# Six norm operations for eight, an inverse on its column factors, and a re-set opening schedule in a fused attention and MoE kernel

## The chip, the cores and the metric

The kernel runs on one core of a Trainium2 chip. Its time is the device time of one execution in microseconds. Three runs of the kernel before gave 586.13, 586.37 and 587.09 us, median 586.37. One profiled execution took 586.01 us, of which the trace shows a span of 584.3 us. TensorE's granted clock is given as a share of 2.4 GHz: 1.00 is 2.4 GHz, 0.50 is 1.2 GHz.

## The reference, cut to what matters

Delta-rule attention for 4 batches and 8 heads over 768 steps with 48 dimensions, and then a two-layer MLP with a squared ReLU on the 3072 rows it gives. `w_in` and `w_out` come as 64-bit floats.

```python
k_n = k / (np.linalg.norm(k, axis=-1, keepdims=True) + 1e-06)
for t in range(S):
    kt, vt, bt = k_n[:, :, t], v[:, :, t], beta[:, :, t, None]
    y[:, :, t] = np.einsum('bhd,bhde->bhe', q[:, :, t], state)
    v_old = np.einsum('bhde,bhd->bhe', state, kt)
    state = state + bt[:, :, :, None] * np.einsum('bhd,bhe->bhde', kt, vt - v_old)
h = np.maximum(x @ w_in, 0.0)          # x: y as 3072 x 384, w_in 384 x 2048
out = (h * h @ w_out).astype(np.float32)
```

## The kernel before, in words

The 768 steps are cut into 12 units of 64, and two units make a pair. Within a unit the recurrence is solved at once: the products of the keys with each other are formed on TensorE, their triangular system is inverted, and TensorE applies the inverse to the values. Two units are prepared together, because their 32 x 32 diagonal blocks are laid out so that one VectorE stream transpose brings all of them into rows (tile `lt`). The inverse is built by substitution, one column per step, two VectorE operations per step.

The first pair (`pair < FAST`) has a shorter path. Its 32 x 32 blocks are inverted as two 16 x 16 blocks each (`invert` on `z16`, 15 steps), scaled by beta over the squared norm (`ended`), transposed into `t1` (L571) and `tt` (L566), and the quarter between the two 16-blocks is then filled in by `corrected`: a first group of products (L588), a scaling with row masks (L594, L597), a second group (L607), a subtraction (L611) and two transposes (L613). `below` then fills the quarter between the two 32-blocks in the same manner (L623, L624, then L633, L634, negated at L638 and L640). `state_part` applies the result to the values (L783), turns the output to the layout of the MLP (`turned_y`, L729) and updates the state (L802).

Products of 64 rows can be put on one of four quarters of the 128 x 128 array: the half of the rows is set by where the inputs lie, the half of the columns by where the output lies. In L588 and L607 inputs and output lie in the same half, which uses two quarters. L430, L688 and L783 also send one head of each pair to the opposite half, which uses all four.

Norms (`prepare`): a square root on ScalarE (L480), then eight small VectorE operations (L485 to L495) for one step of refinement, the division and the beta factor.

The MLP multiplies in two parts per operand, a high and a low half, so each weight has to be split once (`split_weights`): 17 tiles are loaded as 64-bit words, cast on ScalarE or VectorE (L253, into `rest`), joined on VectorE (L279, into `a`), rounded to the high half (L285 or L287), and subtracted for the low half (L269), or, where the table `mode` says P, multiplied by the identity and its negative on TensorE (L265, tile 1 alone). L875 is the first layer, L882 to L885 the squared ReLU and the high half of its result, L850 the low half, L859 the second layer.

All queues are in order and written by hand. In the opening, the string `order` gives the pieces one by one, `fill` and `fillm` say how many weight steps go behind each piece, `loads` the order of the first loads and `ahead` how far weight loads run ahead of the casts. From unit 1 on, pieces of attention are woven into the MLP of the unit before at the fractions in the tables. SP issues every load; a load waits in SP's queue for its buffer, and what stands behind it waits too. Load `kp` (L323) waits for the state update, values `vt` for the end of what used their buffer (in the first pair `goff`, the input of L588), `kb` for the transposes on TensorE that read it (L380).

Of the kernel before, what the change touches and what calls it, by code (L numbers as in the profile page):

```python
# [22 lines left out]
def kernel(  # L23
# [20 lines left out]
              'keys': [0.0259, 0.1552],  # L44
              'm0': 0.0875,
              'm1': 0.9358,
              'prepare': [0.4739, 0.3325],
# [4 lines left out]
              'update': [0.0],  # L52
              'v1': [0.1099, 0.2455],
              'values': [0.2013, 0.7593]},
          2: {'end': 0.0,
              'ended': [0.4457, 0.4449, 0.5557, 0.3799],
              'inverse': [0.042, 0.3114],
              'keys': [0.4933, 0.4581],
              'm0': 0.0151,
              'm1': 0.7158,  # L60
              'out': 0.3937,
# [4 lines left out]
          'ahead': 2,  # L66
# [13 lines left out]
                   'steps': [0.2072, 0.4146, 0.4716, 0.511, 0.6399],  # L80
                   'values': [0, 0.749]},
          'fill': [0, 0, 0, 0, 0, 0, 0, 0, 0, 0, 0, 0, 0, 0, 0, 0, 0, 0, 0, 0, 0, 0, 0, 0, 0, 0, 0, 0, 0, 0, 0, 0, 0, 0, 0,
                   0, 0, 0, 0, 0, 0, 1, 0, 0, 4, 2, 2, 2, 1, 0, 2, 2],
          'fillm': [0, 0, 0, 0, 0, 0, 0, 0, 0, 0, 0, 0, 0, 0, 0, 0, 0, 0, 0, 0, 0, 0, 0, 0, 1, 0, 0, 0, 0, 0, 1, 0, 0, 0, 0,
                    0, 0, 0, 0, 0, 0, 0, 0, 2, 2, 0, 1, 0, 0, 0, 1, 1],
# [3 lines left out]
          'homes': {'0': 'o', '1': 'o', 'b0': 'h', 'c0': 'o', 'k0': 'h', 'k1': 'g', 'w': 'h', 'y': 'o'},  # L89
          'kk': 0,  # L90
          'last': [1, 1],
          'loads': 'kKvbwcwqr',
          'mode': ['AAD', 'AAP', 'AAD', 'AAD', 'AAD', 'AAD', 'AAD', 'AAD', 'AAD', 'AAD', 'AAD', 'DDD', 'AAD', 'AAD', 'AAD',
                   'AAD', 'ADD'],
          'neg': 'DA',
          'odd': {'end': 0.0,
                  'inverse': [0.458, 0.9654],
                  'keys': [0.2429, 0.0785],
                  'm0': 0,
                  'm1': 0.9003,  # L100
                  'out': 0.1651,
                  'prepare': [0.3057, 0.4746],
                  'queries': [0.5785, 0.9867],
                  'rows': [0.9443],
                  'steps': [0.2902, 0.4708, 0.7443, 0.9418],
                  'values': [0.2259, 0.4952]},
          'order': '0A1lBATPPxB2PPPPPPPIGVIIAIBIIIIIIIIIIIeeeGZecccbbyss',
# [3 lines left out]
          'turn': 'DDAAA',  # L111
          'upper': 'DD',
# [245 lines left out]
    def spread_beta():  # L358
# [4 lines left out]
        for i in range(2):  # L363
            for s in range(2):
# [755 lines left out]
```

## Time and profile before

| | us |
|---|---|
| median of three runs | 586.37 |
| profiled execution | 586.01 |
| its span | 584.3 |
| TensorE busy, share of the span | 548.6, 94% |
| VectorE busy | 363.8, 62% |
| ScalarE busy | 318.1, 54% |
| first product of the MLP (L875) | starts at 55.89 |
| last product of the MLP (L900) | ends at 580.5 |

The span is the time from the first to the last recorded instruction, and 1.7 us of the execution lie outside it. A matmul of 32-bit floats shows twice in the trace, so 32 products of the program are 64 records. A busy TensorE at a clock of 0.50 does the same work as at 1.00 in up to twice the time, so its busy share has to be read beside the clock. The opening, to about 92 us, is a chain through all engines; behind it TensorE hardly stops.

### The profile page before, as it was taken

Reading aid. Unit: us, or ns where it says so; the run is one execution under the profiler, and the core shown is the slowest. Engines: PE = TensorE matmul, PEld = TensorE weight load, DVE = VectorE, ACT = ScalarE, POOL = GpSimd, SP = SyncE. Lnnn points to the kernel's source line nnn. Section 1 sums busy time; section 2 is a strip of 40 time slices with the busy share of each in tenths; the row PEclk is TensorE's granted clock in tenths of the full one; section 3 lists DMA queues with packets and bytes.
Section 4 is the critical chain, followed back from the end, with each engine's and each line's share of the span. In section 5 each row is a group of like instructions: output and inputs, shape, how many; then the busy total and the mean of one; then the engine's idle time right before and its main releaser. Section 6 shows DMA issues by size and latency. Waiting matters only on the chain.

```text
span 584.3 us, 20855 instructions
## 1 busy us (share of the span) xinstructions
PE 548.6 (94%) x9344; PEld 525.1 (90%) x9344; DVE 363.8 (62%) x699; ACT 318.1 (54%) x540; POOL 50.5 (9%) x62
## 2 busy tenths in 40 slices
PE   5377869999999999999999999999999999999997
PEld 4366859999899999999999999999999999999997
DVE  1887888995358795458795458794459793420210
ACT  4277876456374455474455474455474455454533
POOL 5110002001002002002001002001002010000000
PEclk9559999999999999999999999999999999999999
DMA  9882970322350230460331450321450320200101
GB/s 172 220 346 51 258 157 2 75 37 30 55 85 2 53 59 14 60 96 2 65 47 15 63 93 2 70 42 19 65 87 2 76 35 4 57 2 2 28 1 27
DMA packets 146793, 37.62 MB, mean 64 GB/s; under 512 B 140400, under 2 KB 143472, under 8 KB 146704
## 3 DMA queue, kind: packets, MB, share of 16 engines
q1 hardware_dynamic: 146624, 36.19, 31.0%
q8 instruction: 73, 1.20, 0.9%
q14 instruction: 16, 0.13, 0.1%
q10 hardware_dynamic: 80, 0.10, 0.0%
HBM read 31.55 MB, written 4.72 MB: 62 GB/s over the span
## 4 chain that ended last, share of the span: by engine, by line
PE 83%; SPq 3%; ACT 2%; DMA 1%; DVE 1%; issue 0%; DVEq 0%; ACTq 0%
PE h L875 34%; PE o L859 31%; PE g L764 3%; PE g L776 2%; PE g L859 2%; PE g L819 2%; PE g L783 2%; SPq L235 2%; PE g L802 1%; PE g L430 1%; PE h L834 1%; SPq L323 1%; DMA w<-in_moe_w_out_dram 1%; PE g L900 1%; PE g L663 1%; PE g L651 1%
## 5 line engine op out<-in xcount | busy, mean ns | idle before, releaser
L859 PE MATMUL o<-w,h_h 128*128 128x384 f32 x704 | 183.7, 341 | 1.2 <-issue 1.1
L875 PE MATMUL h<-x_h,w 128*128 128x256 f32 x1152 | 171.8, 285 | 3.2 <-ACT r L882 3.2
L875 PEld LDWEIGHTS h<-x_h,w 128*128 128x128 f32 x1152 | 153.5, 190 | 6.7 <-ACT r L882 3.7
L850 DVE TENSOR_TENSOR h_l<-r,h_h 128x512 fp32r<-128x512 f32 x96 | 66.4, 692 | 132.9 <-ACT h_h L885 132.9
L859 PEld LDWEIGHTS o<-w,h_h 128*128 128x128 f32 x704 | 122.3, 188 | 4.1 <-issue 1.7
L859 PE MATMUL o<-w,h_l 128*128 128x384 f32 x352 | 118.3, 336 | 1.9 <-DVE h_l L850 1.9
L882 ACT ACTIVATE r<-h 128x512 f32<-128x512 f32 x96 | 57.7, 601 | 104.2 <-PE h L875 92.1
L875 PE MATMUL h<-x_l,w 128*128 128x256 f32 x576 | 100.2, 283 | 0.0
L875 PEld LDWEIGHTS h<-x_l,w 128*128 128x128 f32 x576 | 82.6, 191 | 0.0
L859 PEld LDWEIGHTS o<-w,h_l 128*128 128x128 f32 x352 | 66.1, 188 | 2.6 <-DVE h_l L850 2.5
L883 ACT ACTIVATE r<-r 128x512 f32<-128x512 f32 x96 | 60.8, 633 | 3.1
L885 ACT CAST h_h<-r 128x512 fp32r<-128x512 f32 x96 | 59.6, 621 | 3.0
L541 DVE TENSOR_TENSOR tmp<-lt 128x30 f32<-128x30 f32 (+9 forms) x150 | 53.2, 355 | 3.5
L543 DVE TENSOR_TENSOR lt<-lt,tmp 128x30 f32<-128x30 f32 (+9 forms) x150 | 51.7, 344 | 5.8 <-DVE tmp L541 0.5
L677 POOL TENSOR_SCALAR_AFFINE_SELECT ap<-ap 64x1024 f32<-64x1024 f32 x24 | 33.0, 1374 | 222.0 <-ACT ap L767 219.3
L805 DVE TENSOR_TENSOR qs<-qs,g 48x768 f32<-48x768 f32 x22 | 20.9, 950 | 15.2 <-PE g L802 15.0
L767 ACT COPY ap<-g 128x512 f32<-128x512 f32 x22 | 11.9, 590 | 31.2 <-DVE vt L766 31.0
L482 POOL TENSOR_SCALAR_AFFINE_SELECT lt<-lt 128x1024 f32<-128x1024 f32 x5 | 6.3, 1267 | 219.6 <-ACT s L480 161.9
L822 ACT COPY y<-g 128x768 f32<-128x768 f32 x11 | 8.8, 801 | 27.6 <-PE g L819 27.6
L764 PE MATMUL g<-qs,kt 48*64 48x112 f32 x704 | 19.4, 259 | 0.0
L764 PEld LDWEIGHTS g<-qs,kt 48*64 48x64 f32 x704 | 17.0, 133 | 1.7 <-issue 0.5
L253 ACT CAST rest<-w 128x768 f16<-128x768 bf16 (+1 forms) x16 | 16.4, 1022 | 3.5 <-DMA w<-in_moe_w_out_dram 3.2
(176 smaller groups left out, 617.1 us busy)
## 6 DMA issues: line engine op xcount, KB each, us to landing
w<-in_moe_w_out_dram SPq DMA_DIRECT2D x16, 383.8 KB, 8.2
vt<-in_v_dram SPq DMA_DIRECT2D x48, 96.0 KB, 4.4
kp<-in_k_dram SPq DMA_DIRECT2D x48, 96.0 KB, 3.1
w<-in_moe_w_in_dram SPq DMA_DIRECT2D x6, 767.8 KB, 9.0
out_dram<-rest SPq DMA_DIRECT2D x47, 96.0 KB, 2.2
kb<-in_q_dram SPq DMA_DIRECT2D x40, 64.0 KB, 3.2
kb<-in_k_dram SPq DMA_DIRECT2D x32, 64.0 KB, 2.7
w<-in_moe_w_in_dram SPq DMA_DIRECT2D x3, 511.8 KB, 7.1
```

Of the source, the lines that this page charges most:

```text
L253: (nc.vector.tensor_copy if A["mode"][x][0] == "D" else nc.scalar.copy)(out=head.bitcast(F16)[:, 1::2], in_=raw.rearrange("p n w -> p (n w ...
L541: nc.vector.tensor_tensor(out=tmp, op=ALU.mult, in0=z[:, s:s + 1, s + 1:].broadcast_to([P, nj, nt]), in1=z[:, :nj, s:s + 1].broadcast_to([ ...
L543: nc.vector.tensor_tensor(out=z[:, :nj, s + 1:], in0=z[:, :nj, s + 1:], in1=tmp, op=ALU.add)
L677: nc.gpsimd.affine_select(out=half, in_=half, pattern=[[0, 2 * X], [1, C]], base=0, channel_multiplier=-1, compare_op=ALU.is_gt, fill=0.0)
L764: nc.tensor.matmul(ps[half_rows(b ^ j), j, x], lhsT=kts[u][dims(j), n], rhs=qs[dims(j), n], start=True, stop=True)
L805: nc.vector.tensor_tensor(out=s[dims(j)], in0=s[dims(j)], in1=ps[dims(j)], op=ALU.add)
L850: nc.vector.tensor_tensor(out=h_l, in0=r, in1=h_h.bitcast(F32), op=ALU.subtract)
L859: nc.tensor.matmul(o[i], lhsT=a[:, e, i * P:(i + 1) * P], rhs=w_[w], start=(ft == 0 and n == 0), stop=(ft == FT - 1 and n == 2))
L875: nc.tensor.matmul(hp[:, e], lhsT=half_of(("wi", kt, part))[w][:, f], rhs=x[:, kt], start=(n == 0), stop=(n == 3 * KT - 1))
L882: nc.scalar.activation(out=r, in_=hp, func=AF.Relu)
L883: nc.scalar.activation(out=r, in_=r, func=AF.Square)
L885: nc.scalar.copy(out=h_h, in_=r)
```

## The change

The schedule table is set anew, and the first pair is computed with fewer and smaller operations:

- Norms: the maximum is replaced by a small bias inside the square root; half the root plus the epsilon is formed by a second ScalarE operation, and one VectorE operation adds the refined half. Six VectorE operations remain.
- The inverse starts from the scaled diagonal (`bt` is written there) and is multiplied by the factor of its column from the start, so the two scalings in `ended` go.
- `t1` of the first pair is transposed for the first 16 rows of each block only.
- `corrected` works on 16 columns where it worked on 32, and sends the second head of each pair to the opposite column half. Its scaling for that head becomes four operations on 64 rows, its subtraction three operations where there was one. Two zeroed tiles `w` and `y` take the scaled result.
- Table: `loads` puts the first weight third and the values behind two weights; `ahead` is 4, not 2; tile 1 of the weights no longer goes through TensorE (`mode`); the copies named in `turn`, `neg` and `upper` move partly from VectorE to ScalarE; `fill` and `fillm` put weight steps earlier.

```diff
-          'ahead': 2,
+          'ahead': 4,
-          'loads': 'kKvbwcwqr',
+          'loads': 'kKwbwcvqr',
-          'neg': 'DA',
+          'neg': 'AA',
-          'turn': 'DDAAA',
-          'upper': 'DD',
+          'turn': 'ADAAA',
+          'upper': 'AD',
...
-        nc.scalar.activation(out=s0, in_=n2, func=AF.Sqrt)
+        nc.scalar.activation(out=s0, in_=n2, func=AF.Sqrt, bias=tiny)
+        nc.scalar.activation(out=n1, in_=s0, func=AF.Copy, scale=0.5, bias=1e-6)
...
-        nc.vector.tensor_scalar(out=s1, in0=s0, scalar1=1e-30, scalar2=None, op0=ALU.max)
-        nc.vector.reciprocal(out=s1, in_=s1)
+        nc.vector.reciprocal(out=s1, in_=s0)
         nc.vector.tensor_tensor(out=s1, in0=s1, in1=n2, op=ALU.mult)
-        nc.vector.tensor_tensor(out=s1, in0=s1, in1=s0, op=ALU.add)
-        nc.vector.tensor_scalar(out=n1, in0=s1, scalar1=0.5, scalar2=1e-6, op0=ALU.mult, op1=ALU.add)
+        nc.vector.scalar_tensor_tensor(out=n1, in0=s1, scalar=0.5, in1=n1, op0=ALU.mult, op1=ALU.add)
...
         if d["pair"] < FAST:
             z = z32
-            for h in range(2):
-                r = slice(h * QB, (h + 1) * QB)
-                nc.vector.tensor_tensor(out=z[:, r, r], in0=z16[:, h], in1=bt[:, r].unsqueeze(1).broadcast_to([P, QB, QB]),
-                                        op=ALU.mult)
-                yield
...
-        nc.vector.transpose(out=t1.rearrange("p j i x s -> p s (j i x)"), in_=z.rearrange("p s t -> p (s t)"))
+        ns = HB if d["pair"] else QB
+        nc.vector.transpose(out=t1[..., :ns].rearrange("p j i x s -> p s (j i x)"),
+                            in_=z[:, :ns].rearrange("p s t -> p (s t)"))
...
-                    nc.tensor.matmul(ps[j][r, 0, x], lhsT=goff[r, j, x].rearrange("p n t -> p (n t)"), rhs=t1[r, j, i, x],
+                    nc.tensor.matmul(ps[j][half_rows(b ^ j), 0, x, :QB], lhsT=goff[r, j, x].rearrange("p n t -> p (n t)"), rhs=t1[r, j, i, x, :QB],
                                      start=True, stop=True)
...
-                    nc.tensor.matmul(ps[r, j, 0, x], lhsT=yt[j][r, x].rearrange("p n s -> p (n s)"), rhs=z[r, j, x],
+                    nc.tensor.matmul(ps[half_rows(b ^ j), j, 0, x, QB:], lhsT=yt[j][r, x].rearrange("p n s -> p (n s)"), rhs=z[r, j, x, QB:],
                                      start=True, stop=True)
...
-        nc.vector.tensor_tensor(out=z[:, :, :, QB:], in0=z[:, :, :, QB:], in1=ps[:, :, 0, :, QB:], op=ALU.subtract)
+        nc.vector.tensor_tensor(out=z[:, 0, :, QB:], in0=z[:, 0, :, QB:], in1=ps[:, 0, 0, :, QB:], op=ALU.subtract)
+        for b in range(2):
+            part = z[half_rows(b), 1, :, QB:]
+            nc.vector.tensor_tensor(out=part, in0=part, in1=ps[half_rows(1 - b), 1, 0, :, QB:], op=ALU.subtract)
```

On VectorE, between the scaling in the first `corrected` and its subtraction, stand weight steps (`a` joins a weight, `w_...` is its low half). Before:

```order
L594 TENSOR_SCALAR tmp<-o,rows 128x8x32 x2
L279 SCALAR_TENSOR_TENSOR a<-w_142,rest 128x768
L269 TENSOR_TENSOR w_464<-a,w_464 128x768
L279 SCALAR_TENSOR_TENSOR a<-w_224,rest 128x768
L611 TENSOR_TENSOR tt<-tt,g 128x2x8x16
L613 STREAM_TRANSPOSE t_410<-tt 128x256 x2
```

And now, with the line numbers of the changed kernel:

```order
L601 TENSOR_SCALAR y<-o,rows 64x8x16 x4
L280 SCALAR_TENSOR_TENSOR a<-w_126,rest 128x768
L280 SCALAR_TENSOR_TENSOR a<-w_132,rest 128x768
L270 TENSOR_TENSOR w_459<-a,w_459 128x768
L280 SCALAR_TENSOR_TENSOR a<-w_217,rest 128x768
L617 TENSOR_TENSOR tt<-tt,g 128x8x16
L620 TENSOR_TENSOR tt<-tt,g 64x8x16 x2
L622 STREAM_TRANSPOSE t_373<-tt 128x256 x2
```

Four weight steps stand there instead of three, and the scaling and the subtraction are in more pieces.

On TensorE, between the second group of `corrected` (L607) and the first of `below` (L623), stood the low half of weight tile 1:

```order
L607 MATMUL g<-tt,tmp 64x32 x2
L265 MATMUL g<-a,eye 128x384
L265 MATMUL g<-w_468,minus 128x384
L265 MATMUL g<-a,eye 128x384
L265 MATMUL g<-w_468,minus 128x384
L623 MATMUL g<-tt,mt 32x32
L624 MATMUL g<-t_410,mt 32x32
```

Now the two groups stand back to back:

```order
L613 MATMUL g<-tt,w 64x16 x2
L613 MATMUL g<-tt,y 64x16 x2
L632 MATMUL g<-tt,mt 32x32
L633 MATMUL g<-t_373,mt 32x32
```

The four products of 384 columns have left the engine; their subtraction is done on VectorE.

On SP, the loads from weight tile 9 on, counted from 0 (`kb` keys of unit 3, `kp` keys by rows, `vt` values, `w_...` weights). Before:

```order
L235 DMA w_241<-in_moe_w_out_dram 128x1535 x2
L329 DMA kb<-in_k_dram 64x16x48 x2
L323 DMA kp<-in_k_dram 64x8x48 x4
L235 DMA w_892<-in_moe_w_out_dram 128x1535 x2
L323 DMA vt<-in_v_dram 64x8x48 x4
L235 DMA w_1006<-in_moe_w_out_dram 128x1535 x2
L235 DMA w_1015<-in_moe_w_in_dram 128x2047
L235 DMA w_1035<-in_moe_w_in_dram 128x2047
L235 DMA w_1043<-in_moe_w_in_dram 128x2047
L323 DMA vt<-in_v_dram 64x8x48 x4
L235 DMA w_1056<-in_moe_w_out_dram 128x1535 x2
L235 DMA w_1076<-in_moe_w_out_dram 128x1535 x2
```

And now:

```order
L236 DMA w_237<-in_moe_w_out_dram 128x1535 x2
L236 DMA w_240<-in_moe_w_out_dram 128x1535 x2
L330 DMA kb<-in_k_dram 64x16x48 x2
L324 DMA vt<-in_v_dram 64x8x48 x4
L236 DMA w_787<-in_moe_w_out_dram 128x1535 x2
L324 DMA kp<-in_k_dram 64x8x48 x4
L236 DMA w_862<-in_moe_w_in_dram 128x2047
L236 DMA w_906<-in_moe_w_in_dram 128x2047
L236 DMA w_1014<-in_moe_w_in_dram 128x2047
L236 DMA w_1034<-in_moe_w_out_dram 128x1535 x2
L236 DMA w_1043<-in_moe_w_out_dram 128x1535 x2
L324 DMA vt<-in_v_dram 64x8x48 x4
```

One more weight tile stands ahead of the keys of unit 3, and the second load of values stands behind the last weight instead of ahead of the last two.

On ScalarE, the cast of the first weight now stands between the copies of the transposed keys of unit 1 and the second copies of `z`; before, the first cast stood behind the copy of the query products (L691).

## Rows read from the trace of the kernel before

**Rows 1.** Page, part 4: shares of the chain that ended last, by engine.

```profile
PE 83%; SPq 3%; ACT 2%; DMA 1%; DVE 1%; issue 0%; DVEq 0%; ACTq 0%
```

**Rows 2.** Windows: stretch, then busy us of each engine, clock, DMA share, GB/s.

```profile
44.00:56.00 12.00, 8.63 (x458) 7.68 (x458) 7.99 (x12) 8.49 (x14) 0.00 (x0) 1.00 0.22 43
...
56.00:92.00 36.00, 28.61 (x526) 25.74 (x527) 29.25 (x43) 29.44 (x50) 1.27 (x1) 1.00 0.71 175
...
92.00:584.00 492.00, 486.94 (x7999) 470.95 (x7997) 298.00 (x579) 258.87 (x435) 36.57 (x31) 1.00 0.24 41
```

**Rows 3.** Chain of waits, 60 to 100 us: start us, us, what.

```profile
75.93 5.06 DMA w<-in_moe_w_out_dram
...
81.07 1.04 ACT rest L253
```

**Rows 4.** Timeline of VectorE, 15 to 43 us: start us, us, operation [idle before].

```profile
17.30 0.18 DVE L485 TENSOR_SCALAR s<-s 128x32 f32<-128x32 f32 x1 [0.32 <-ACT s L480]
...
29.79 0.76 DVE L555 TENSOR_TENSOR w<-w,bt 128x256 f32<-128x256 f32 x2
...
30.59 1.99 DVE L571 STREAM_TRANSPOSE t<-w 128x1024 f32<-128x1024 f32 x1
...
37.18 0.95 DVE L279 SCALAR_TENSOR_TENSOR a<-w,rest 128x768 int32<-128x768 int32 x1
...
40.78 0.42 DVE L611 TENSOR_TENSOR tt<-tt,g 128x256 f32<-128x256 f32 x1 [0.39 <-PE g L607]
```

**Rows 5.** Timeline of TensorE, 27 to 57 us.

```profile
27.49 1.99 PE L688 MATMUL g<-qs,kt 48*64 48x64 f32 x64 [1.16 <-ACT kt L385]
...
32.72 3.62 PE L588 MATMUL o<-t,vt 64*64 64x32 f32 x64 [3.25 <-DVE t L571]
...
37.06 0.42 PE L607 MATMUL g<-tt,m 64*64 64x32 f32 x4 [0.72 <-ACT m L597]
...
40.66 1.65 PE L265 MATMUL g<-a,eye 128*128 128x384 f32 x2
...
44.13 0.21 PE L623 MATMUL g<-tt,mt 32*32 32x32 f32 x1
...
47.12 1.27 PE L783 MATMUL h<-vt,tt 64*64 64x48 f32 x64
...
53.94 2.02 PE L588 MATMUL g<-t,vt 64*64 64x32 f32 x64
...
55.89 0.97 PE L875 MATMUL h<-x_h,w 128*128 128x256 f32 x6
```

**Rows 6.** Windows of 1 us, for the granted clock.

```profile
16.00:17.00 1.00, 0.00 (x0) 0.00 (x0) 0.97 (x1) 0.31 (x1) 0.00 (x0) 0.87 0.95 336
...
39.00:40.00 1.00, 1.00 (x24) 1.00 (x22) 1.00 (x2) 1.00 (x2) 0.00 (x0) 0.50 0.99 396
...
44.00:45.00 1.00, 0.88 (x65) 0.64 (x64) 0.61 (x1) 0.76 (x2) 0.00 (x0) 0.98 0.00 0
```

**Rows 7.** Timeline of ScalarE: the second copies of z, the negations.

```profile
12.73 0.37 ACT L442 COPY z<-g 128x256 f32<-128x256 f32 x1 [1.25 <-PE g L430]
...
46.19 0.78 ACT L640 ACTIVATE tt<-h 32x256 f32<-32x256 f32 x2
```

**Rows 8.** DMA issues begun between 6 and 10 us, last column us to landing.

```profile
w<-in_moe_w_in_dram SPq DMA_DIRECT2D x1, 767.8 KB, 4.9
```

**Rows 9.** Timeline of the SP queue, 54 to 62 us.

```profile
54.13 3.13 SPq L323 DMA_DIRECT2D kp<-in_k_dram  x4
...
58.51 3.29 SPq L323 DMA_DIRECT2D vt<-in_v_dram  x4
```

**Rows 10.** Waits between 56 and 92 us: us, times, longest.

```profile
PE h L875 <- ACT r L882: 3.2, 2, 2.7
...
PE o L859 <- DVE h_l L850: 1.9, 2, 1.2
...
PE g L633 <- ACT m L626: 1.8, 1, 1.8
```

More of the change, by code (lines that the diff above doesn't have):

```diff
@@ L43 @@
               'inverse': [0.4545, 0.9674],
-              'keys': [0.0259, 0.1552],
-              'm0': 0.0875,
+              'keys': [0.0259, 0.15],
+              'm0': 0.0942,
               'm1': 0.9358,
-              'prepare': [0.4739, 0.3325],
+              'prepare': [0.4761, 0.3194],
               'queries': [0.945, 0.8623],
@@ L51 @@
               'steps': [0.3132, 0.5592, 0.7964, 0.8486],
-              'update': [0.0],
-              'v1': [0.1099, 0.2455],
-              'values': [0.2013, 0.7593]},
+              'update': [0.0647],
+              'v1': [0.2624, 0.2455],
+              'values': [0, 0.7871]},
           2: {'end': 0.0,
-              'ended': [0.4457, 0.4449, 0.5557, 0.3799],
+              'ended': [0.3926, 0.4449, 0.5557, 0.3799],
               'inverse': [0.042, 0.3114],
               'keys': [0.4933, 0.4581],
-              'm0': 0.0151,
+              'm0': 0.0164,
               'm1': 0.7158,
-              'out': 0.3937,
+              'out': 0.3959,
               'queries': [0.6885, 0.6959],
@@ L356, in load_beta @@
                 nc.sync.dma_start(out=brows[r0:r0 + X], in_=by[j, b * X:(b + 1) * X])
+    yts = []
     def spread_beta():
@@ L370, in spread_beta @@
         nc.scalar.copy(out=betas, in_=global_ps.rearrange("p (d t) -> p d t", t=HB))
+        for name in ("w", "y"):
+            y = apool.tile([P, XD * 2], F32, name=name)[:, :X * C].rearrange("p (x n s) -> p x n s", x=X, n=2)
+            nc.gpsimd.memset(y[..., QB:].rearrange("p x n s -> p (x n) s"), 0.0)
+            yts.append(y)
         return betas
@@ L587, in corrected @@
                     r = half_rows(b)
-                    nc.tensor.matmul(ps[j][r, 0, x], lhsT=goff[r, j, x].rearrange("p n t -> p (n t)"), rhs=t1[r, j, i, x],
+                    nc.tensor.matmul(ps[j][half_rows(b ^ j), 0, x, :QB], lhsT=goff[r, j, x].rearrange("p n t -> p (n t)"), rhs=t1[r, j, i, x, :QB],
                                      start=True, stop=True)
-        yt = [apool.tile([P, 2 * X * HB], F32, name=name).rearrange("p (x n s) -> p x n s", x=X, n=2) for name in ("m", "tmp")]
+        yt = yts
         for j in range(2):
             for n in range(2):
-                if j and A["yt"][i] == "D":
-                    nc.vector.tensor_scalar(out=yt[j][:, :, n], in0=ps[j][:, 0], scalar1=rows[:, 2 + n:3 + n], scalar2=None,
-                                            op0=ALU.mult)
-                else:
-                    nc.scalar.mul(out=yt[j][:, :, n], in_=ps[j][:, 0], mul=rows[:, 2 + n:3 + n])
+                for b in range(1 + j):
+                    to, of = (half_rows(b), half_rows(1 - b)) if j else (slice(P), slice(P))
+                    dst, src, by = yt[j][to, :, n, :QB], ps[j][of, 0, :, :QB], rows[to, 2 + n:3 + n]
+                    if j and A["yt"][i] == "D":
+                        nc.vector.tensor_scalar(out=dst, in0=src, scalar1=by, scalar2=None, op0=ALU.mult)
+                    else:
+                        nc.scalar.mul(out=dst, in_=src, mul=by)
         if not i:
```

44 lines of the change are left out of this document (23 added, 21 removed).

## The prediction

> **What bounds the kernel now.** I read the shares of the chain that ended last first: TensorE holds 83% of it [rows 1]. The windows say where it does not. From 92 us to the end of the span TensorE is busy for 486.9 of 492.0 us, and most of the 5.1 us left is the tail behind its last product; from 56 to 92 us it is busy for 28.6 of 36.0 [rows 2]. So time won in the opening is kept to the end, at the same amount, and time won off TensorE's path later is worth nothing. The chain of waits shows what holds the stretch to 92 us: it runs through the loads, and the last weight lands at 75.93 + 5.06 = 81.0 us, with its cast on ScalarE right behind, at 81.07 [rows 3]. The waits of that stretch show the price: TensorE stood for 3.2 + 1.9 + 1.8 = 6.9 us for results of ScalarE and VectorE [rows 10], engines that are in order and were standing behind casts of weights not yet there. Before 56 us the chain is the arithmetic of the first pair; its steps are in the timelines of VectorE and TensorE [rows 4, 5].
>
> **The first pair, up to its correction.** Two VectorE operations of 0.18 us go from the norms, about 0.4 with their gaps; the added ScalarE operation runs beside the reciprocal. The two scalings behind the inverse go: 29.79 to 30.59, 0.8. The transpose to `t1` halves: 1.99 to 1.0, an estimate by its elements; the bounds are 1.99 and 0.8. Together 2.2, so the correction begins at 30.5 instead of 32.72 [rows 4, 5]. The later pairs keep their own scaling, and their shorter norms lie beside a busy TensorE: nothing.
>
> **The two groups of products.** The first took 3.62 us at a clock of 0.50, and the second ran from 37.06 to 40.66 [rows 5], 3.6. No row has 16 columns on four quarters. The nearest are on four quarters with more columns: 64 records of 64 columns in 1.99 us in the same slow stretch, and 64 of 48 columns in 1.27 at full clock, where the same kernel's own two-quarter group of 32 columns took 2.02 [rows 5]. So fewer than 2.0 and no more than 3.6; I take 2.0, by the nearest row, 1.6 off each group.
>
> A rule speaks against this. The Trainium skill ("TensorE: Matmul & The Clock Gate", Part 3, The mechanism) says that a weight load overlaps a running product only when the two use different row groups, and the column half, which is what changes here, does not enter. By that rule both groups stay at 3.6. The rows above disagree: 48 columns on four quarters were faster than 32 on two. I go by the rows and keep the rule as a rival.
>
> **Scaling, subtraction and what stands between.** Four scalings for two, and three subtractions of half the columns for one of 0.42 [rows 4]: between 0 and 0.9 each; I take 0.4 and 0.5. The second group then ends at 30.5 + 2.0 + 1.3 + 2.0 = 35.8 against 40.7. VectorE is the later one now: it has four weight steps of about 0.9 [rows 4] between scaling and subtraction, so the subtraction begins at 33.8 + 3.6 = 37.4 and the transposes end at about 39.1, where they ended at 42.0. The next group of TensorE had to wait further, behind the four products of L265, from 40.66 to 44.13 [rows 5]; they are gone. So it begins at 39.1: **5.0 us earlier**, and what VectorE has in their place (one subtraction, 0.9) lies behind it.
>
> **The clock.** This is what I hold against the 5.0. The granted clock fell to 0.50 near 17 us, when TensorE had been without work; it was still 0.50 in the microsecond from 39 to 40, with TensorE busy throughout on the second group; and it was 0.98 from 44 to 45 [rows 6], right behind the four 128 x 384 products that the change removes. What raised it before is therefore not there any more, and the products now standing from 30 to 56 us are small ones with waits between. I expect 1.2 GHz up to the MLP. Between 44 and 56 us TensorE did 8.6 us of work at full clock [rows 2]. The 64 records of 32 columns took 3.62 against 2.02, 1.8 times as long [rows 5]. Of the 8.6, the second unit's first correction group (2.02) gets its four quarters and stays at about 2.0; some 1.0 of transposes runs beside other waits; the remaining 5.6 grow by 0.8 of themselves, 4.5. The negation for the second head moves from VectorE to ScalarE, behind the first, which takes 0.78 [rows 7]; between 0 and 0.8 of it is new on the path, since VectorE's own ended a little later than ScalarE's, and I take 0.5. So the MLP's first product comes at 55.89 - 5.0 + 4.5 + 0.5, about where it was. At the half clock the MLP then does half its work until the clock returns; between 0 and 4 us are lost, I take 2.0. The second unit's second correction group loses columns and halves in the same way: 0.8 won.
>
> The Trainium skill's section on the clock gate in the same page (Part 1) has the engine throttled by default and released by activity; the trace agrees in that small products at 39 us had not released it.
>
> **The loads.** SP's queue was blocked before by the `kp` load, which waited for the state update until 54.13; then keys, a weight, values, a weight, three narrow weights, values and two weights went out [rows 9], 27 us until 81.0. Now one more weight is out before, values stand behind the first correction of unit 1 (near 53.5), and the second values stand behind the last weight. By 768 KB a weight [rows 8] and the sizes in the order, about a fifth of the bytes is gone from that stretch, so the last weight lands near 53.5 + 21.5 = 75, 6 us earlier, or near 71.5 where the row loads cost more than their bytes. ScalarE and VectorE no longer stand behind missing weights, and of the 6.9 us of waits [rows 10] I take 6.0 as gone. VectorE has room: 29.3 of 36.0 busy [rows 2]. Its next limit, if the loads come, is that list of weight steps itself, and TensorE's own work: 28.6 us in that stretch cannot shrink.
>
> **Sum.** 0.0 at the first MLP product, -2.0 clock, +0.8, +6.0: 4.8 us. Against the profiled execution 586.01 - 4.8 = 581.2; the median of the runs is 0.36 above it, so **581.4 us**. By the unknowns (groups of products, pieces, clock, waits) from 579 to 584.
>
> **Rivals.**
>
> *The clock comes back early.* If the products on four quarters, or those of the turn (L729), bring 2.4 GHz back before the MLP, the 4.5 and the 2.0 are not paid, and the second unit's first group is 0.9 shorter; of this some 2.0 is given back, because VectorE's weight steps then end later than TensorE needs them. Gain 4.8 + 4.5 + 2.0 + 0.9 - 2.0 = 10.2, about 576. For it: TensorE no longer waits 3.5 us for itself. Against: the microsecond from 39 to 40.
>
> *The quarters give nothing.* Both groups stay at 3.6: the second ends at 39.0, the subtraction and transposes at 40.7, 1.6 later, and unit 1 loses its 0.8. Gain 4.8 - 1.6 - 0.8 = 2.4, 584. The rule of the skill named above would have it so.
>
> *The waits stay.* The loads come earlier, but VectorE's list of splits, which was 81% busy in that stretch, has no place to move to, and TensorE waits for low halves (L850) as before. Then 6.0 falls to about 0.5: 0 - 2.0 + 0.8 + 0.5, a loss of 0.7 against 586.4: 587, no change.
>
> *Slower: the half clock lasts into the MLP.* The MLP's first 36 us are woven with small products and waits, and each microsecond at 0.50 loses half a microsecond of its work. The gains behind 56 us, 6.8, are used up after 14 us at half clock, that is when the clock is not back by 70; to 80 it would be 591. For it: the same windows. Against: the MLP's products are of the large kind that stood before the rise at 44. A second way to it, the cast of the first weight on ScalarE, does not decide: it stands ahead of copies that began at 12.73 [rows 7], the weight is now issued right behind the two loads of keys with which the program begins, and before it landed 4.9 us after its issue with loads ahead of it as well [rows 8]; each microsecond by which it makes the copies late costs one.
>
> **Chances.** Forecast (579 to 584) 0.47; clock back early (574 to 579) 0.24; no help from quarters, or smaller gains to 585.2, 0.11; waits stay, within 0.2% (585.2 to 587.5, what a measurement here can tell from no change) 0.07; slower 0.11. Faster 0.82, same 0.07, slower 0.11. The range of 8 in 10 leaves out half of each end: 575.5 to 585.4.
>
> **What would show it.** In the changed profile: L592's first group at about 30.5 for 2.0 us (3.6: the quarters give nothing); L632 at 39; the clock in the windows from 40 to 56 (0.50: forecast; 1.00: first rival); the first product of L884 at 55 to 56, or 51; the last cast of a weight at 71 to 76; and TensorE's waits from 56 to 92 at about 1 us. I am wrong in the mechanism if the last weight still lands at 81, or if TensorE has new idle time behind 92 us.

## The result, and the profile after

The changed kernel took 577.61 us (median of four runs, 576.72 to 578.85) beside 586.73 us (586.13 to 587.90) for the kernel before on the same chip: ratio 0.985, 95% interval 0.982 to 0.987. That is faster, by 9.1 us where the forecast's sum had 4.8. It lies inside the range of 8 in 10 (575.5 to 585.4), but below the forecast's own band (579 to 584), in the band that was given to an early return of the clock (574 to 579); that rival is not what happened, as the clock below shows. The profiled execution took 578.17 us with a span of 576.4, 7.9 below that of before; the steps below are counted in spans.

The chain that ended last (page, part 4, shares by engine) is now TensorE for 91%, before it was 83% with 3% of SP's queue [rows 1]:

```profile
PE 91%; DVE 5%; DMA 1%; ACT 1%; issue 1%; SPq 0%; DVEq 0%
```

The windows (busy us of PE, PEld, DVE, ACT and POOL, then clock, DMA share, GB/s), in the same stretches as [rows 2]:

```profile
44.00:56.00 12.00, 9.25 (x389) 8.02 (x388) 11.51 (x17) 10.37 (x21) 0.00 (x0) 0.64 0.58 135
56.00:92.00 36.00, 35.82 (x566) 33.79 (x566) 31.96 (x57) 28.20 (x49) 1.43 (x2) 0.86 0.48 123
92.00:576.00 484.00, 480.17 (x7958) 465.12 (x7956) 287.86 (x554) 256.52 (x434) 33.83 (x30) 1.00 0.24 41
```

From 56 to 92 TensorE was idle for 0.2 us where it had been for 7.4, but its clock there is 0.86 on the mean. The timeline of TensorE, to hold against [rows 5]:

```profile
32.85 1.91 PE L592 MATMUL o<-t,vt 64*64 64x16 f32 x64 [6.67 <-DVE t L574]
...
35.50 0.40 PE L613 MATMUL g<-tt,w 64*64 64x16 f32 x4 [0.75 <-ACT w L603]
...
40.42 0.31 PE L632 MATMUL g<-tt,mt 32*32 32x32 f32 x2 [2.11 <-DVE tt L617]
...
55.52 1.65 PE L884 MATMUL h<-x_h,w 128*128 128x256 f32 x6
```

The first group of the correction takes 1.91 us at the half clock, for 3.62. It begins at 32.85, no earlier than before. The MLP's first six products take 1.65 us where they took 0.97, at half the clock. Windows of 1 us show how that came (the clock is the third number from the end), and the clock records of the trace give the times behind them:

```profile
45.00:46.00 1.00, 0.51 (x40) 0.38 (x29) 1.00 (x2) 0.66 (x2) 0.00 (x0) 0.78 0.11 22
...
49.00:50.00 1.00, 0.94 (x64) 0.96 (x64) 0.99 (x3) 1.00 (x2) 0.00 (x0) 0.50 0.06 8
...
60.00:61.00 1.00, 1.00 (x9) 0.78 (x10) 0.14 (x1) 0.00 (x0) 0.00 (x0) 0.50 0.79 261
...
66.00:67.00 1.00, 1.00 (x38) 0.87 (x39) 0.94 (x4) 0.15 (x1) 0.00 (x0) 1.00 0.99 367
```

TensorE had 1.2 GHz from 18.1 to 45.4, 2.4 GHz to 48.8, 1.2 GHz again to 65.9, then 2.4 GHz. Before, 2.4 GHz had come back at 44.0 and stayed.

VectorE and GpSimd, 27 to 32 us, show what was not forecast: two operations of the inverse take four times as long as their neighbours, while GpSimd masks the query products (sets half of each block to zero) beside them.

```profile
27.20 0.28 DVE L536 TENSOR_TENSOR tmp<-t,w 128x110 f32<-128x110 f32 x1
27.51 1.09 DVE L538 TENSOR_TENSOR w<-w,tmp 128x110 f32<-128x110 f32 x1
28.64 1.15 DVE L536 TENSOR_TENSOR tmp<-t,w 128x96 f32<-128x96 f32 x1
29.82 0.26 DVE L538 TENSOR_TENSOR w<-w,tmp 128x96 f32<-128x96 f32 x1
...
31.66 1.04 DVE L574 STREAM_TRANSPOSE t<-w 128x512 f32<-128x512 f32 x1
```

```profile
27.33 2.36 POOL L686 TENSOR_SCALAR_AFFINE_SELECT ap<-ap 64x1024 f32<-64x1024 f32 x2 [1.86 <-ACT ap L700]
```

Last, the weights: SP's queue, then ScalarE's casts of the last two weights, then TensorE's longest waits from 56 to 576 (us, times, longest).

```profile
60.91 2.90 SPq L236 DMA_DIRECT2D w<-in_moe_w_out_dram  x4
63.90 4.07 SPq L324 DMA_DIRECT2D vt<-in_v_dram  x4
```

```profile
73.61 1.08 ACT L254 CAST rest<-w 128x768 f16<-128x768 bf16 x1
75.06 1.11 ACT L254 CAST rest<-w 128x768 f16<-128x768 bf16 x1
```

```profile
PE h L884 <- ACT r L891: 0.2, 1, 0.2
PE g L785 <- issue: 0.2, 1, 0.2
```

The last weights go out from 60.9 to 63.8, ahead of the second values, and no cast behind 56 waits for a load; before, the last one landed at 81.0 [rows 3], and TensorE's waits were 6.9 us [rows 10].

### The profile page after: what moved, and what is told of

Its sections match the earlier page's. It is cut to its first block, busy times and chain, and to the rows that moved or that the text cites. A ratio compares the mean times of both kernels' runs of the same rounds, so it can differ in the third digit from the quotient of the medians.

```text
span 576.4 us, 20843 instructions
## 1 busy us (share of the span) xinstructions
PE 546.3 (95%) x9338; PEld 525.5 (91%) x9338; DVE 359.9 (62%) x690; ACT 317.9 (55%) x547; POOL 47.6 (8%) x63
## 4 chain that ended last, share of the span: by engine, by line
PE 91%; DVE 5%; DMA 1%; ACT 1%; issue 1%; SPq 0%; DVEq 0%
PE h L884 37%; PE o L868 32%; PE g L773 3%; PE g L785 2%; PE g L868 2%; PE g L792 2%; PE g L828 2%; PE g L811 2%; PE g L437 2%; PE h L843 1%; PE o L387 1%; DVE tmp L536 1%; DVE w L538 1%; PE g L909 1%; DVE lt L484 1%
## 5 line engine op out<-in xcount | busy, mean ns | idle before, releaser
L884 PE MATMUL h<-x_h,w 128*128 128x256 f32 x1152 | 174.3, 288 | 0.2 <-ACT r L891 0.2
L884 PEld LDWEIGHTS h<-x_h,w 128*128 128x128 f32 x1152 | 155.5, 193 | 3.3 <-issue 0.9
L859 DVE TENSOR_TENSOR h_l<-r,h_h 128x512 fp32r<-128x512 f32 x96 | 68.9, 718 | 139.8 <-ACT h_h L894 139.8
L894 ACT CAST h_h<-r 128x512 fp32r<-128x512 f32 x96 | 59.6, 621 | 3.0
L548 DVE TENSOR_TENSOR tmp<-lt 128x30 f32<-128x30 f32 (+9 forms) x150 | 49.4, 329 | 3.6
L686 POOL TENSOR_SCALAR_AFFINE_SELECT ap<-ap 64x1024 f32<-64x1024 f32 x24 | 30.4, 1268 | 219.4 <-ACT ap L776 216.7
L773 PE MATMUL g<-qs,kt 48*64 48x112 f32 x704 | 19.4, 259 | 0.0
L846 ACT CAST x_h<-h 128x384 fp32r<-128x384 f32 x22 | 9.5, 484 | 12.3 <-PE h L843 12.3
```

Of the source, the lines that this page charges most:

```text
L548: nc.vector.tensor_tensor(out=tmp, op=ALU.mult, in0=z[:, s:s + 1, s + 1:].broadcast_to([P, nj, nt]), in1=z[:, :nj, s:s + 1].broadcast_to([ ...
L686: nc.gpsimd.affine_select(out=half, in_=half, pattern=[[0, 2 * X], [1, C]], base=0, channel_multiplier=-1, compare_op=ALU.is_gt, fill=0.0)
L773: nc.tensor.matmul(ps[half_rows(b ^ j), j, x], lhsT=kts[u][dims(j), n], rhs=qs[dims(j), n], start=True, stop=True)
L859: nc.vector.tensor_tensor(out=h_l, in0=r, in1=h_h.bitcast(F32), op=ALU.subtract)
L884: nc.tensor.matmul(hp[:, e], lhsT=half_of(("wi", kt, part))[w][:, f], rhs=x[:, kt], start=(n == 0), stop=(n == 3 * KT - 1))
L894: nc.scalar.copy(out=h_h, in_=r)
```

## Where the time went, in three stretches

For the two kernels and each experiment I cut the profiled span at two instructions that all have: the first product of the MLP, and ScalarE's third rounding of its hidden layer (L885 before, L894 after), at which all weights are in. A is the opening, B the MLP's start with the last weights, C the rest, in us; the ratio is to the kernel before, from five to twelve runs of each (four of the changed kernel).

| kernel | A | B | C | span | clock back for good | ratio |
|---|---|---|---|---|---|---|
| before | 55.9 | 28.1 | 500.3 | 584.3 | 44.0 | 1 |
| after | 55.5 | 22.5 | 498.4 | 576.4 | 65.9 | 0.985 |
| e1 same half | 58.0 | 21.7 | 498.0 | 577.7 | 60.6 | 0.992 |
| e2 tile 1 on TensorE | 58.4 | 21.2 | 500.3 | 579.9 | 59.7 | 0.991 |
| e3 idle products | 63.4 | 20.5 | 498.6 | 582.5 | 65.0 | 0.995 |
| e4 mask later, extra tile | 53.2 | 23.0 | 494.0 | 570.2 | 64.1 | 0.976 |
| e5 old loads | 57.0 | 24.1 | 500.2 | 581.4 | 74.0 | 0.997 |
| e6 new operations, old table | 52.8 | 30.0 | 500.5 | 583.3 | 63.3 | 0.995 |
| e7 old operations, new table | 62.1 | 21.9 | 498.7 | 582.6 | 65.8 | 0.998 |
| e8 extra tile alone | 55.1 | 23.0 | 493.2 | 571.2 | 65.1 | 0.979 |
| e9 mask later alone | 54.8 | 20.6 | 498.3 | 573.7 | 56.1 | 0.984 |
| e10 mask later, all at 64 | 55.2 | 22.6 | 498.5 | 576.2 | 65.9 | 0.984 |
| e11 mask later, weights 64, x 32 | 54.2 | 23.0 | 493.6 | 570.8 | 64.9 | 0.976 |
| e12 weights 64, x 32 | 56.2 | 21.5 | 495.1 | 572.8 | 57.4 | 0.979 |

The gain of 7.9 us is 0.4 in A, 5.6 in B and 1.9 in C. The forecast had 0.0, 4.8 (-2.0 + 0.8 + 6.0) and 0. Repeated runs of one kernel spread over 1 to 10 us (10 in e3), so a single profile's tenths in A and B mean little; the ratios carry the verdicts. The profiled run of e1 is its fastest, 3.8 us below its median.

The cut between B and C does not fall at the same place of TensorE's own work: 101 of the MLP's 2880 products have begun there before, 91 after, 78 in e5. Counted by these products, the changed kernel leads by 0.4 us at the first, by 5.6 at the 200th and still at the 400th, by 7.3 at the 500th, and by 7.9 at the last.

TensorE's idle time from 56 to 92 us, from windows as above, is the plainest sign of the weights: 7.4 us before, 0.2 after, 6.6 in e6, 2.0 in e5, 0.9 in e7.

## The experiments

**e6 and e7: operations and table apart.** e6 is the changed code with the old table, e7 the old code with the changed table.

```diff
-    A = {... 'order': '0A1lBTPBAP2xPPPPPIPIPIVIBIIIIAIIIIIIIeGeecZecGcbybss', ...}
+    A = {... 'order': '0A1lBATPPxB2PPPPPPPIGVIIAIBIIIIIIIIIIIeeeGZecccbbyss', ...}
```

> The changed kernel's operations (six norm operations, inverse on its column factors, half of t1, 16 columns on four quarters) with the table of the kernel before. Theory (the table carries the gain by its loads and its list of weight steps, as the run with the old loads suggests): TensorE's waits of 5 to 7 us between 56 and 92 stay, the opening is 1 to 3 us shorter and meets weights that are not there: ratio 0.994 to 1.000, 583 to 587. Rival (the operations shorten the opening by 5 us and the MLP starts that much earlier): 0.988 to 0.992.

> The kernel before with the changed table alone: old norms, scalings, whole t1, 32 columns on two quarters. Theory (as for the run with the new operations and the old table): the waits between 56 and 92 go, the opening is 3 to 5 us longer than in the changed kernel, at half clock: ratio 0.990 to 0.995, 581 to 584. Rival (the table is right only for the shorter operations): 1.000 or more.

Measured: e6 0.995 (0.993 to 0.997), e7 0.998 (0.996 to 1.000): 2.8 and 1.2 us, where both together give 9.0. e6 came as its theory had it. e7 is slower than its theory (0.990 to 0.995), and its interval touches the rival's 1.000: its waits went as expected, but its opening is 6.6 us longer than in the changed kernel and not 3 to 5. The table of stretches says why the sum is more than its parts. e6's opening is 3.1 us shorter, and there its first group stands at the time that the prediction had for the changed kernel:

```profile
30.59 1.90 PE L591 MATMUL o<-t,vt 64*64 64x16 f32 x64 [1.10 <-DVE t L573]
```

But the weights are not there. SP's queue, ScalarE's last cast, and TensorE's two largest waits from 56 to 92 of e6:

```profile
64.20 4.61 SPq L323 DMA_DIRECT2D vt<-in_v_dram  x4
68.85 5.26 SPq L235 DMA_DIRECT2D w<-in_moe_w_out_dram  x4
```

```profile
79.86 1.05 ACT L253 CAST rest<-w 128x768 f16<-128x768 bf16 x1 [0.97 <-DMA w<-in_moe_w_out_dram]
```

```profile
PE h L883 <- ACT r L890: 4.0, 2, 3.1
PE o L867 <- DVE h_l L858: 1.9, 2, 1.1
```

The time won up to the MLP is spent waiting there: B is 30.0. e7 has the weights in time (B 21.9), but its opening is 6.2 us longer than before, for its long operations run at the half clock and the table puts weight steps between them; its first group:

```profile
34.40 3.63 PE L589 MATMUL o<-t,vt 64*64 64x32 f32 x64 [7.73 <-DVE t L572]
```

Operations without the table win time that the loads give back; the table without the operations wins the loads and loses the opening.

**e5: only the first loads and the look-ahead undone.**

```diff
-          'ahead': 4,
+          'ahead': 2,
-          'loads': 'kKwbwcvqr',
+          'loads': 'kKvbwcwqr',
```

> The changed kernel (ratio to the kernel before 0.985) with the table's loads and ahead as before the change: the first weight behind the values again, two weights ahead instead of four. Loads theory (TensorE's 6.9 us of waits between 56 and 92 went because the weights come earlier): the last weight lands at about 81 again, waits of 5 to 6 us come back there, ratio 0.993 to 0.996, 582 to 584. Rival (what removed the waits is the table's setting of the weight steps and of the modes, the loads are early enough either way): under 1.5 us, ratio 0.985 to 0.988.

Measured: 0.997 (0.995 to 0.999), so these two entries are dear, dearer than the theory had it, but for the most part not in the way it said: of the 7.2 us of idle time that the change removed between 56 and 92, 2.0 came back, in one wait. SP's queue, ScalarE's last cast and that wait:

```profile
63.80 2.87 SPq L236 DMA_DIRECT2D w<-in_moe_w_out_dram  x4
67.35 5.40 SPq L324 DMA_DIRECT2D vt<-in_v_dram  x4
```

```profile
78.19 1.09 ACT L254 CAST rest<-w 128x768 f16<-128x768 bf16 x1
```

```profile
PE g L642 <- ACT m L635: 2.0, 1, 2.0
```

The last weights still go out ahead of the second values, at 63.8. What else is lost begins in A: the new order of pieces has ScalarE cast the first weight early, and with the old loads that weight is late. The cast waits for it, and the copies of `z` behind it wait too:

```profile
13.90 1.05 ACT L254 CAST rest<-w 128x768 f16<-128x768 bf16 x1 [2.66 <-DMA w<-in_moe_w_in_dram]
```

So the transpose ahead of the norms begins at 17.13 and not 15.09, and A is 1.5 longer. B is 1.6 longer with that wait in it, and 1.2 GHz lasts until 74.0 (but for 67.2 to 70.6). The 1.8 in C are mostly the cut: by products, e5 is 4.5 us behind the changed kernel at the 200th and 4.9 at the end. So `ahead` and the first loads are worth 4.5 us in the opening and the MLP's start, and most of the removal of the waits is not theirs. That the rest of it comes from the place of the values in SP's queue fits e5 and e6; no run moves that place alone.

**e1: quarters.** The second heads back on the column half of their own rows; scaling and subtraction read them there.

```diff
-   nc.tensor.matmul(ps[j][half_rows(b ^ j), 0, x, :QB], lhsT=goff...
+   nc.tensor.matmul(ps[j][half_rows(b), 0, x, :QB], lhsT=goff...
...
-   nc.tensor.matmul(ps[half_rows(b ^ j), j, 0, x, QB:], lhsT=yt...
+   nc.tensor.matmul(ps[half_rows(b), j, 0, x, QB:], lhsT=yt...
```

> The changed kernel (577.6 us), with the second heads of both groups of the first correction put back on the column half of their own rows; still 16 columns, the same number of instructions. Quarters theory: the first group takes 3.6 us at a clock of 0.50 as before the change (1.91 now), the second group some 1 to 1.6 us more, and the second unit's group at 51.5 about 0.9 more: 580.5 to 581.5. Rival (the 16 columns instead of 32 made it shorter, the quarters give nothing): the first group stays at 1.9, and the time at 577.6 within 0.5.

Measured: 0.992 (0.989 to 0.995), 4.5 us over the changed kernel; the theory had 3 to 4. The row that decides, beside the 1.91 of the changed kernel:

```profile
32.86 3.60 PE L592 MATMUL o<-t,vt 64*64 64x16 f32 x64 [6.36 <-DVE t L574]
```

Same columns, same count, same clock of 0.50, 3.60 us for 1.91: the quarters nearly halve the group, and the 16 columns alone give nothing (3.62 with 32, [rows 5]).

**e4 and e9: the mask later.** ScalarE's copy of the query products, and with it GpSimd's mask, waits for the 13th step of the inverse. e4 does it with a new tile of two elements, e9 with a tile that is there.

```diff
-        nc.scalar.copy(out=ap[0], in_=ps)
         yield
+        nc.scalar.copy(out=warm[:, 1:], in_=z16[:, 0, 0, 13:14])
+        nc.scalar.copy(out=ap[0], in_=ps)
         masked(u)
...
-          'order': '0A1lBTPBAP2xPPPPPIPIPIVIBIIIIAIIIIIIIeGeecZecGcbybss',
+          'order': '0A1lBTPBAP2xPPPPPIPIPIVIBIIIIAGIIIIIGIIeeecZeccbybss',
```

This is e9; in e4 the first copy goes to the new tile.

> The changed kernel with ScalarE's copy of the first query products, and so GpSimd's two mask operations on it, put behind the 13th of 15 steps of the inverse (a copy of two elements of its result makes ScalarE wait): the masks then lie beside VectorE's transposes of t1 and tt. Theory (GpSimd's mask stretches VectorE's two-input operations beside it): the two operations of 1.09 and 1.15 us in the inverse go back to 0.27, the transpose of t1 begins at 30.0 instead of 31.7, and everything behind it up to the MLP 1.7 earlier: 576. Rival 1 (something else stretches them): unchanged, 577.6. Rival 2 (the opening gets shorter, but VectorE's weight steps, 97% busy from 28 to 60, take it back): the transpose at 30.0, the time at 577 to 577.6.

> The later mask without the extra tile: the element that makes ScalarE wait is copied into the unused half of a tile that is there, so every address is as in the changed kernel. Theory: the inverse's two stretched operations back at 0.27 us, 1.9 us less up to the MLP, and no growth behind: ratio 0.981 to 0.982. Rival 1 (the growth belongs to the mask): 0.976. Rival 2 (nothing): 0.985.

Measured: e4 0.976 (0.974 to 0.979), e9 0.984 (0.981 to 0.986). VectorE and GpSimd of e4:

```profile
27.30 0.27 DVE L538 TENSOR_TENSOR w<-w,tmp 128x110 f32<-128x110 f32 x1
27.61 0.26 DVE L536 TENSOR_TENSOR tmp<-t,w 128x96 f32<-128x96 f32 x1
...
29.73 1.07 DVE L574 STREAM_TRANSPOSE t<-w 128x512 f32<-128x512 f32 x1
```

```profile
29.91 2.35 POOL L686 TENSOR_SCALAR_AFFINE_SELECT ap<-ap 64x1024 f32<-64x1024 f32 x2 [4.68 <-ACT ap L703]
```

The same two operations are back at 0.27, the transpose begins 1.9 us earlier, and beside the mask the transposes keep their length (1.07 for 1.04). That the mask stretched them is shown. From the start of the transpose ahead of the norms (L484) to the first group it takes 16.1 us in each of the five runs whose mask lies elsewhere (e4, e6, e9, e10, e11), and 17.8 in the changed kernel. In the whole time, the 1.7 us do not arrive in full: e9 gives 0.001 and not the 0.003 expected, e11 against e12 below 0.003, and no pair is clear of its intervals. The clock can account for a part: in e9, e10 and e11 2.4 GHz did not come before 56, and from L633 to the MLP's first product it took 14.5 to 14.9 us, against 13.6 to 14.0 in the changed kernel, e4 and e8, which had a spell of 2.4 GHz there. e4 won more than the mask could: its lead over the changed kernel grew all the way to the end, C is 4.3 us shorter. That was the next question.

**e8, e10, e12, e11: addresses.** e8 has e4's extra tile and not its mask; it moves `m`, the staging tiles, `x_h`, `x_l` and the hidden layer's tiles by 32 bytes. e10 to e12 add a pad of 32 bytes ahead of `kp`, which moves the weights.

```diff
+        late_ = apool.tile([P, 2, 1], F32, name="late")
+        nc.gpsimd.memset(late_, 0.0)
...
+    pad = const.tile([P, 8], F32, name="pad")
+    nc.gpsimd.memset(pad, 0.0)
```

e8 has the first, e10 the second, e11 and e12 both.

> The changed kernel with one more tile of 8 bytes a partition in SBUF, which nothing reads; it moves the tiles behind it (m, a, rest, x_h, x_l, r, h_h, h_l) by 32 bytes, from addresses that leave 32 over a multiple of 64 to multiples of 64. In the run with the later mask, which had such a tile too, products of the MLP's first layer followed each other by 116 to 119 ns instead of 120 to 121, and its lead over the changed kernel grew from 1.9 us at 62 to 6.2 at the end. Address theory: the 4 us of that growth are here, without the later mask: ratio 0.977 to 0.979. Rival (they came of the mask or of chance): 0.985.

> The later mask, and a pad of 32 bytes ahead of kp, so that all tiles behind it, the weights too, begin at multiples of 64 (in the run with the extra tile the weights did not). Address theory, if it is the moving operand x_h and x_l alone that counts: as the first run with the later mask, ratio 0.976. If the weights' addresses count as well: 0.970 to 0.974. Rival (addresses do nothing): 0.981.

> The later mask, with 32 bytes of padding ahead of kp and the unused tile ahead of m: the weights at multiples of 64, x_h and x_l at 32 over one; so the two operands of the MLP's products differ by 32 as they do in the pad run (weights at 32, x_h at 0), where the spacing was 119 ns on the mean, and not as in the run with all at 0 or in the changed kernel with both at 32 (121). Theory (the difference of the two addresses counts): 119 ns, ratio 0.974 to 0.978. Rival (x_h's own address counts): 121 ns, 0.982 to 0.984.

> The same addresses as in the run before it (weights at multiples of 64, x_h and x_l at 32 over one), the mask where the changed kernel has it. Difference theory: ratio 0.978 to 0.980, that is 1.9 us or 0.003 above the run with the later mask. Rival: 0.985.

Measured, with the remainders of the tiles' addresses by 64 bytes:

| | weights | x_h, x_l | mask | ratio (95%) |
|---|---|---|---|---|
| after | 32 | 32 | early | 0.985 (0.982, 0.987) |
| e8 | 32 | 0 | early | 0.979 (0.976, 0.982) |
| e12 | 0 | 32 | early | 0.979 (0.976, 0.982) |
| e9 | 32 | 32 | later | 0.984 (0.981, 0.986) |
| e10 | 0 | 0 | later | 0.984 (0.981, 0.986) |
| e4 | 32 | 0 | later | 0.976 (0.974, 0.979) |
| e11 | 0 | 32 | later | 0.976 (0.973, 0.978) |

e10 refuted the first reading, in which the address of `x_h` and `x_l` alone counts (0.976 expected, 0.984 measured). In all four arrangements it is the difference of the two addresses that goes with the time, not either one. The tiles around them move with them, so only the spacing ties it to the MLP's products. First the changed kernel, then e8, first-layer products behind each other in the quiet tail:

```profile
501.87 0.88 PE L884 MATMUL h<-x_h,w 128*128 128x256 f32 x6
...
502.95 0.88 PE L884 MATMUL h<-x_h,w 128*128 128x256 f32 x6
```

```profile
497.46 0.86 PE L886 MATMUL h<-x_h,w 128*128 128x256 f32 x6
...
498.50 0.86 PE L886 MATMUL h<-x_h,w 128*128 128x256 f32 x6
```

From one group of six to the next, with three of `x_l` between, nine products: 1.08 us or 120 ns each, and 1.04 or 116 ns. The MLP has 12 x 16 x 9 = 1728 of them. Over all of them behind 100 us the means are 120.9 to 121.1 ns in every kernel with equal remainders and 118.3 or 118.4 in e4, e8, e11 and e12. That is 2.7 ns each, 4.7 us in all, and C is 3.3 to 5.2 us shorter in these four than in the changed kernel. **e11 and e4, at 0.976 or some 573 us, beat both kernels**; pairs with and without the later mask (e4 and e8, e11 and e12) differ by 0.003, some 1.6 us, inside their intervals.

**e2 and e3: the clock.** e2 gives TensorE back the four products of 384 columns; e3 lays products of the identity, whose results are overwritten, into its idle stretches.

```diff
-          'mode': ['AAD', 'AAD', 'AAD', ...
+          'mode': ['AAD', 'AAP', 'AAD', ...
...
+    def hold(ps, n):
+        for _ in range(n):
+            nc.tensor.matmul(ps[:, :SH + P], lhsT=plus, rhs=eye, start=True, stop=True)
```

> The changed kernel with the low half of weight tile 1 back on TensorE (four products of 384 columns). Clock theory: these products lie in TensorE's idle stretch of 38 to 42 us, the clock comes back to 1.00 by 44 and stays there as in the kernel before, the 16 us at 0.50 between 49 and 65.5 are not seen, and the MLP's first 16 us run up to 8 us faster, of which VectorE's list of weight steps lets through a part: 573 to 576, in spite of up to 2 us more ahead of the first product of below. Rival (the products only stand in the way, and the clock falls at 49 again): 578.5 to 580.

> The changed kernel with idle products added on TensorE (168 columns of the identity, results overwritten) where it waits: 30 ahead of the transposes of the queries, 7 ahead of the query products, 40 ahead of the first correction's first group, 4 ahead of its second, 14 ahead of below, 7 ahead of the first unit's values. Clock theory: the clock stays at 1.00 from 17 to 66 us; on the chain of the opening the groups at 32.9, 35.5, 41.5, 42.5 and 44.4 take half, some 3.9 us less, and the 16 us at 0.50 in the MLP's start up to 8 less, with 3 to 5 given back to VectorE's weight steps: 568 to 572. Rival (VectorE, 97% busy from 28 to 60 us, sets the pace, TensorE's speed there is worth nothing): 576 to 578. If the clock falls all the same, the idle products stand in the way: 578 to 581.

Measured: e2 0.991 (0.989 to 0.993), e3 0.995 (0.992 to 0.998), both slower than the changed kernel, and slower than their rivals had it too; the clock theory failed in both. In e2 1.2 GHz lasted to 46.1 and came again from 49.5 to 59.7; A is 2.9 us longer with the four products, and C 1.9. In e3 the idle products delayed the opening by 7.9 us and did not hold the clock. Its windows:

```profile
28.00:29.00 1.00, 0.26 (x2) 0.26 (x3) 0.90 (x4) 1.00 (x3) 0.95 (x2) 1.00 1.25 292
29.00:30.00 1.00, 1.00 (x27) 0.91 (x30) 0.86 (x5) 1.00 (x3) 0.64 (x1) 1.00 0.72 252
30.00:31.00 1.00, 1.00 (x61) 0.93 (x52) 1.00 (x2) 0.80 (x4) 0.00 (x0) 0.93 0.96 375
31.00:32.00 1.00, 1.00 (x6) 1.00 (x7) 1.00 (x1) 0.93 (x1) 0.00 (x0) 0.50 1.01 353
```

TensorE was idle for 1.2 us, from 27.6 to 28.7, then busy without a gap; the clock fell at 30.9 and stayed at 1.2 GHz until 51.3, with TensorE busy all that time. What I argued about the four products, that they had brought the clock back at 44, is not shown: a rise to 2.4 GHz came at 46.1 and 46.2 in e2 and e6, which have them, and between 43.6 and 47.0 in the changed kernel, e1, e4, e5 and e8, which do not; and in e2 and e6 the clock fell again at 49.5 and 53.1. What steers it here stays open. What the half clock costs in the MLP can be read from two pairs with nearly the same instructions. e4 had 10.9 us of 1.2 GHz behind its first MLP product, e9 1.3, and their B are 22.96 and 20.63; e11 had 10.7, e12 1.2, and their B are 22.95 and 21.48. That is 2.3 and 1.5 us for some 9.5 us, about a quarter of a microsecond for each or less.

## Why the prediction was right, and where its sizes were off

In one sentence: the large gain, the waits for the weights, was forecast with its reason; the opening came out at the forecast time because two errors met; and the gain behind 92 us was not seen.

- **The first pair up to the correction.** Forecast 30.5, measured 32.85, later than before. The missing term is the mask. In the new order the query products come earlier, and the mask on them fell beside the inverse: 0.82 + 0.89 = 1.7 us, shown by e4; e7 has it too with the old operations: two stretched operations of 1.21 and 1.16, and 19.4 us from the transpose ahead of the norms to the first group, where the kernel before has 17.7. It was priced at nothing because I asked what the operations cost, and not what would run beside them. A page of the Trainium skill would have told me to look: "SBUF — State Buffer", section "SBUF: two separate sides", has GpSimd, where it reads SBUF, and a VectorE operation with two SBUF inputs exclude each other for a whole instruction. The trace agrees: two stretched operations, 1.09 and 1.15 us, beside a mask of two parts in 2.36. Without the mask the pair gains 1.6 us, not 2.2 (16.1 for 17.7): scalings and `t1` gave their 0.8 and 0.95, but up to the operation that multiplies by `bt` only 0.1 was won and not 0.4, and that operation takes 1.15 for its pair where the old one took 0.76. It now reads `bt` from a strided diagonal; that this is why was not tested alone. That e6 has the first group at 30.59, the forecast time, is partly luck: its transpose ahead of the norms began 0.5 earlier than before.
- **Quarters.** Forecast 2.0, measured 1.91, and e1 gives the price of being wrong: 3.60. The rival by the Trainium skill's rule on row groups ("TensorE: Matmul & The Clock Gate", Part 3, The mechanism) falls. The second group, forecast at 2.0, ran from 35.50 to 38.31, 2.8, since it waits for the scaling between; in e6, which starts it later, it took 1.91. The four scalings took 1.46 us where two took 0.88 in e7, 0.6 more (forecast 0.4), the three subtractions 0.88 for 0.42 (forecast 0.5 more).
- **Up to the MLP.** `below` began at 40.42 with L632 and at 41.53 with its partner L633, not at 39.1: the delay above. The first product of the MLP came at 55.52 for 55.9. Here two errors met, and that it fits is luck: 2.6 us were won up to L633 and not 5.0, and 2.2 were paid behind it (14.0 us for 11.8) and not 5.0, with the clock at 2.4 GHz from 45.4 to 48.8.
- **Half clock in the MLP's start.** Forecast -2.0, and the changed kernel had 10.4 us of 1.2 GHz there. The two pairs above give 1.5 to 2.3 us for some 9.5. So the term was about right, but the rate in the slower rival, half a microsecond for each, was too high, and its limit of 70 too early. The +0.8 of unit 1's second group cannot be read apart, since the MLP's products are woven into it.
- **The waits.** Forecast +6.0, measured 7.2 of idle time gone (7.4 to 0.2). Together with the clock this gives B, 5.6 where 4.8 was forecast. The reason was right, weights out ahead of the second values, and e6 against the changed kernel shows that the table does it. The path was not quite the one I gave: the first values went out at 48.5 and not at 53.5, for they waited for the products that read unit 0's values (L792), not for unit 1's first correction; the last weight was issued by 63.8, and the last cast at 75.06 stands at the forecast landing time without waiting for a load.
- **Behind 92 us.** I said that nothing would change there. TensorE's idle time in C fell from 6.5 to 4.4 us, which is the size of the 1.9. Three waits of the kernel before make up most of it and are gone after. Two, of 0.7 and 0.5 us at 86.1 and 90.5, are for VectorE's low half and ScalarE's result. The third, at 153, lies between two products of the second layer, and the trace names no releaser:

```profile
154.11 0.61 PE L859 MATMUL o<-w,h_h 128*128 128x384 f32 x2 [1.10 <-issue]
```

It was in the rows that I had: of the 5.1 us idle behind 92, the tail is 3.8, and I priced the rest at nothing. e2 has such a wait of 1.09 at 149, e6 one of 0.99 at 152, and none of the other kernels has one; these are the three in which tile 1's four products stand on TensorE. Whether they bring it, and how, is open. The two lengths of C, 498 and 500, go with this wait, and in e5 with the cut.

With +0.4, +5.6 and +1.9 for 0.0, +4.8 and 0 the forecast came out 3 us too cautious on the profiled run; the last 1.3 of the difference between the medians is scatter of both kernels' runs. The sum itself has a slip: 586.01 - 4.8 + 0.36 is 581.6, not 581.4, which decides nothing.

## What to carry to other kernels

Price a change of operations and a change of the order of loads together: here the operations alone gave 2.8 us, the order alone 1.2, hardly clear of nothing, and both 9, since time won ahead of a wait for data is spent in that wait. When an instruction moves to an earlier time, look at what runs beside it on the other engines then, here GpSimd beside VectorE. In e5 a cast that the order moves forward stood 2.7 us for its load, and the copies behind it stood with it. And an experiment that adds a tile moves addresses: pad it, or run the padding alone as well, before its time is put down to what it was meant to test.

## What the runs showed of the hardware that was not expected

- Two VectorE operations with two SBUF inputs took 1.09 and 1.15 us for 0.27 beside GpSimd's mask; the transposes beside it in e4 kept their length (1.07 for 1.04). GpSimd's memsets, which read nothing, lay beside the same kind of operations from 23.1 to 25.1 us and stretched none (0.25 to 0.29).
- First-layer products of 256 columns followed each other by 121 ns on the mean when weights and moving operand had the same remainder by 64 bytes (0 and 0, 32 and 32) and by 118.3 or 118.4 when it differed by 32 (either way round): some 4.7 us of the whole kernel. Products of the second layer stayed at 173 to 174 ns in all.
- 32 products of 64 rows by 16 columns took 1.91 us on four quarters and 3.60 on two, at 1.2 GHz, with the same row halves in the same order.
- In e3 the granted clock fell at 30.9 us, under a TensorE that had worked for 2.2 us after 1.2 us of idleness, and stayed at 1.2 GHz for 20 us of work without a gap; in executions of nearly the same program (e4, e9) it came back for good 8 us apart.
- TensorE stood for 1.0 to 1.1 us near 150 us, where the trace names no releaser (before, e2) or VectorE's update of the state (e6), in the three kernels that have tile 1's four products on TensorE, and in no other.
